# One core: attention scores in float32 for sixteen heads from operands of 128 rows, and a new fixed order of the whole program

## The chip, the cores and the metric

The program runs on one core of one Trainium2 chip. The time is what the device takes for one execution, in microseconds (us); lower is better. A core has five engines that run side by side, each through its own list of instructions in order: PE (TensorE, matrix multiplication; PEld is its loading of weights), DVE (VectorE), ACT (ScalarE), POOL (GpSimd) and SP (SyncE, which here only issues DMAs). PE's results go to PSUM; the other operands lie in SBUF, a memory of 128 partitions (rows).

## The reference

An attention with decay over 8 batches, 8 heads, 576 positions and 64 channels, and then a two-layer product with a cosine gate over the 4608 tokens.

```python
scores = scale * np.matmul(q, k.transpose(0, 1, 3, 2))
log_f = np.log(np.clip(f, 0.0001, 1.0))
cum = np.cumsum(log_f, axis=-1)
decay = cum[:, :, :, None] - cum[:, :, None, :]
scores = np.where(causal, -1000000000.0, scores + decay)
attn = softmax(scores)
x = (attn @ v) as (4608, 512)
h = x @ w_in                      # 512 -> 2048
out = (h * np.cos(h)) @ w_out     # 2048 -> 512
```

q, k, v and f are float32; both weights arrive as 64-bit floats.

## The kernel before

**The work.** Heads are taken in pairs, n = 0 to 31, four pairs to a batch. The first four pairs (n < N32 = 4) run `attention32`, all in float32; pairs 4 to 7 (n < NQ = 8) run `attention` with float32 scores; the other 24 run `attention` with scores from two products of rounded operands (L975 and L976). After each four pairs comes the two-layer product for that batch, in two halves of 320 and 256 tokens: `gemm1` (L1072, PE, three float16 products for each block) makes h, four steps on ACT and DVE (L1087 to L1093) make h times cos(h), L1100 and L1101 (or L1102) split it into two float16 parts g, and `gemm2` (L1118) multiplies these with the second weights.

**The float32 scores.** `load32` (L754 to L763) fills an operand tile for a head: 64 rows of q and k (L759, a DMA into partitions 0 to 63), 4 rows of decay (L760, a DMA into partitions 64 to 67, from a buffer `cum_d` in device memory), and 64 columns of zeros set by POOL (L758). The products are L818 (pairs 0 to 3) and L973 (pairs 4 to 7) and contract over 68 rows. The decay rows come out of a chain of their own at the start: load f (L586), clip, logarithm, running sum and split (L587 to L593), write to `cum_d` (L597).

**The weights.** The 32 tiles of the weights arrive as 64-bit words (L627, 512 KB each). DVE turns each into float32 in three steps (L617, L621, L625), ACT takes a bound of it (L636), and when a group's scale is known, ACT and DVE split it into two float16 parts (L646, L653). All 16 tiles of the second weights must be there before their scale is.

**v.** `prep_vscale` loads the four pairs of a batch once for a scale (L709, into a `stage` buffer), and `attention32` and `attention` load them again for the work (L769 or L906, buffer `v2`, two of them).

**The buffers.** Raw tiles of the second weights, the float32 operands of pairs 0 to 3 and g share a ring of 8 buffers named `g`; raw tiles of the first weights use `h`; the float32 operands of pairs 4 to 7 use `stage`.

**What sets the order.** Every operation is entered in a plan (`Plan.op`) with its engine, a cost and what it reads and writes. `order` runs a simulated schedule three times and then shifts due times by the table SHIFT; the last pass sets the place of each operation on its engine. Some operations have a second engine (`alt`): DVE or POOL for the subtractions, ACT or DVE for the copies out of PSUM (L777 and L778). Where PE is expected to wait in the first 200 us (FILL), the plan puts in pads: products of constant tiles (L1186) into a PSUM buffer that is about to be written, with no use for the result. The class `Clock` is the plan's picture of PE's clock, which in the profile is either 1.0 or 0.5 of full speed.

## Time and profile before

The time before is 1072.21 us, the median of 3 runs (1070.8 to 1072.59).

| | us |
|---|---|
| median of the runs | 1072.21 |
| the profiled execution, its own time | 1073.1 |
| its span, from the first to the last instruction | 1071.4 |
| PE busy | 1050.1 |
| ACT busy | 832.2 |
| DVE busy | 819.7 |
| POOL busy | 155.3 |
| pads, L1186 | 158 of them |

How to read the profile: a row names the line of the kernel, the engine, the operation, what it writes and reads, how often, the busy time in us and the mean of one in ns. The idle time is that of the engine just before these instructions, with what it waited for. A float32 product shows as two records, so 32 records are 16 products. Mean granted clock is given as PEclk. The tables by stretches give each engine's busy time with the number of records in brackets.

### The profile page before, as it was taken

How to read it: one execution, taken by the hardware profiler on the slowest of the kernel's cores; microseconds unless marked ns; L12 is line 12 of the kernel's file. 1: busy time of each engine (PE TensorE's matmuls, PEld its weight loads, DVE VectorE, ACT ScalarE, POOL GpSimd, SP SyncE). 2: the span in 40 equal slices, each digit the busy share in tenths (PEclk: the TensorE clock that was granted, in tenths of full speed). 3: DMA queues.
4: the chain of work that ended last, by engine and by line, in shares of the span. 5: the costliest groups of instructions: out<-in, count | busy, mean ns of one | idle time of the engine just before them, and what ended most of it. 6: DMA issues, size and time to landing. Idle time of an engine off the chain costs nothing. (4 is left out here: it accounts for less than half of the span.)

```text
span 1071.4 us, 23498 instructions
## 1 busy us (share of the span) xinstructions
PE 1050.1 (98%) x8975; PEld 841.6 (79%) x8975; DVE 819.7 (77%) x1801; ACT 832.2 (78%) x1739; POOL 155.3 (14%) x271
## 2 busy tenths in 40 slices
PE   8999999899999999999999999999999999999998
PEld 4778776688778887788778877778778877788787
DVE  6989999677887979678886879778776868671613
ACT  4758989588887989788888979887877978762522
...
PEclk9999999799999999999999999999999999999999
...
GB/s 267 309 284 109 99 135 102 126 162 158 180 152 147 139 142 167 149 101 159 182 154 144 127 148 167 169 129 130 178 144 144 134 142 75 85 59 21 7 20 20
DMA packets 256280, 146.37 MB, mean 137 GB/s; under 512 B 223337, under 2 KB 231529, under 8 KB 256169
## 3 DMA queue, kind: packets, MB, share of 16 engines
...
## 5 line engine op out<-in xcount | busy, mean ns | idle before, releaser
L1118 PE MATMUL hp<-g,W2s 128*128 128x256 f16 (+1 forms) x3072 | 390.9, 287 | 0.6 <-DVE W2s L653 0.4
L1072 PE MATMUL hp<-xh,W1s 128*128 128x256 f16 (+1 forms) x2048 | 380.4, 286 | 1.1 <-ACT h L1078 1.1
L1118 PEld LDWEIGHTS <-W2s 128*128 128x128 f16 x3072 | 297.9, 98 | 78.0 <-issue 0.8
L1072 PEld LDWEIGHTS <-W1s 128*128 128x128 f16 x3072 | 295.9, 98 | 78.6 <-issue 1.7
L1072 PE MATMUL hp<-xl,W1s 128*128 128x256 f16 (+1 forms) x1024 | 292.6, 286 | 0.0
L1013 DVE SCALAR_TENSOR_TENSOR PS<-pa,ri,PS 128x576 f16<-128x576 f32 (+2 forms) x280 | 140.7, 544 | 32.1 <-ACT PS L1009 31.3
L992 ACT ACTIVATE pa<-pa,nb 128x576 f32<-128x576 f32 (+2 forms) x280 | 141.1, 506 | 19.8 <-DVE nb L987 18.6
L987 DVE CUSTOM_DVE_ANT_0 pa<-pa,mask 128x576 f32<-128x576 f32 (+2 forms) x280 | 131.5, 513 | 31.8 <-PE pa L976 26.1
L1009 ACT ACTIVATE PS<-pa,ri 128x576 f16<-128x576 f32 (+2 forms) x280 | 134.1, 545 | 15.0 <-DMA pt<-PS 9.7
L1078 ACT ACTIVATE h<-hp 128x320 f32<-128x320 f32 (+1 forms) x256 | 101.3, 416 | 36.6 <-PE hp L1072 36.0
L1093 DVE TENSOR_TENSOR h<-h,r 128x1280 f32<-128x1280 f32 (+1 forms) x64 | 89.1, 1392 | 41.4 <-ACT r L1091 41.2
L997 POOL TENSOR_SCALAR ri<-L 128x1 f32<-128x1 f32 (+1 forms) x168 | 46.8, 279 | 410.4 <-ACT pa L992 404.9
L921 POOL TENSOR_TENSOR QK<-stage,QK 64x576 fp32r<-64x576 f32 x46 | 77.3, 1680 | 170.5 <-issue 116.4
L1091 ACT ACTIVATE r<-r,halfpi,m_inv 128x1280 f32<-128x1280 f32 (+1 forms) x64 | 86.2, 1347 | 18.8 <-DVE r L1089 18.3
L1101 DVE TENSOR_TENSOR g<-h,g 128x1280 f16<-128x1280 f32 (+1 forms) x62 | 84.2, 1358 | 14.1 <-ACT g L1100 13.7
L1087 DVE TENSOR_SCALAR r<-h,m_a 128x1280 int32<-128x1280 f32 (+1 forms) x64 | 56.8, 888 | 49.3 <-ACT h L1078 48.3
L1089 DVE SCALAR_TENSOR_TENSOR r<-r,m_b,h 128x1280 f32<-128x1280 int32 (+1 forms) x64 | 91.3, 1426 | 0.7
L975 PE MATMUL pa<-QK 128*128 128x288 f32 (+4 forms) x288 | 90.3, 330 | 1.5 <-DVE PS L1013 1.5
L1100 ACT CAST g<-h 128x1280 f16<-128x1280 f32 (+1 forms) x64 | 74.2, 1159 | 15.1 <-DVE h L1093 14.9
L1124 ACT ACTIVATE ot<-hp,m_o 128x320 f32<-128x320 f32 (+1 forms) x64 | 32.3, 504 | 65.9 <-PE hp L1118 50.4
L1042 PEld LDWEIGHTS <-vv 128*64 128x64 f16 x1512 | 69.4, 111 | 16.9 <-issue 14.2
L1042 PE MATMUL pa<-pt,vv 128*64 128x256 f16 (+2 forms) x1512 | 78.8, 256 | 3.7 <-DMA pt<-PS 3.4
(118 smaller groups left out, 1166.7 us busy)
## 6 DMA issues: line engine op xcount, KB each, us to landing
...
```

Of the source, the lines that this page charges most:

```text
L975: T.matmul(c, hi[:, 0, isl], hi[:, 1, d], start=True, stop=False)
L987: op("DVE", c_dve(w) + 0.008, lambda view=view, ib=ib, o=o, w=w, mk=mk, c=c: V.tensor_tensor_reduce(out=view(ib, o, w), in0=view(ib, o, w) ...
L992: op("ACT", c_act(w, True, 2), lambda view=view, ib=ib, o=o, w=w, c=c: A.activation(view(ib, o, w), view(ib, o, w), AF.Exp, bias=nb.get()[ ...
L1009: op("ACT", c_act(w, True, 1), lambda view=view, ib=ib, o=o, w=w, c=c, out_=out_: A.activation(out_(0), view(ib, o, w), AF.Copy, scale=ri. ...
L1013: op("DVE", c_dve(w) + 0.06, lambda view=view, ib=ib, o=o, w=w, c=c, out_=out_: V.scalar_tensor_tensor(out_(1), view(ib, o, w), ri.get()[: ...
L1042: T.matmul(d, vv.get()[:, jb, hd, kv], m, start=first and x == 0, stop=last and x == 2)
L1072: T.matmul(hp.get()[:, 0:w_], WS_[1][:, at(1, 4 * c + cb), w, fs], x.get(), start=(n == 0), stop=(n == 11))
L1078: op("ACT", c_act(w_, True), lambda hp=hp, k=k: A.activation(h.get()[:, k, 0:w_], hp.get()[:, 0:w_], AF.Copy, scale=float(2.0 ** -24)), re ...
L1089: op("DVE", c_dve(N) + 0.045, lambda: V.scalar_tensor_tensor(fl(r), fl(r).bitcast(I32), b1.get()[:, c:c + 1], fl(h), op0=ALU.mult, op1=ALU ...
L1091: op("ACT", c_act(N, aps=2), lambda: A.activation(fl(r), fl(r), AF.Sin, scale=inv.get()[:, c:c + 1], bias=halfpi), reads=[inv], writes=[r] ...
L1093: op("DVE", c_dve(N), lambda: V.tensor_tensor(fl(h), fl(h), fl(r), op=ALU.mult), reads=[r], writes=hk, prio=pr)
L1118: T.matmul(po.get()[:, 0:w_], WS_[2][:, at(2, 4 * c + k), w, msl], gh.get()[:, i, k, 0:w_], start=(n == 0), stop=(n == 47))
```

## The change

- **Operands of 128 rows.** The host packs q and k of batches 0 and 1 (pairs 0 to 7) into a new array `qk2` of 128 rows a head: rows 0 to 3 zero, rows 4 to 67 q and k, rows 68 to 127 zero. `load32` loads all 128 rows with one DMA (576 KB in place of 288 KB), and the decay rows are then written over rows 0 to 3. The products contract over 128 rows in place of 68, and the decay DMA now also waits for the load that it overwrites. POOL clears 128 rows in place of 68.
- **v of batch 0 once.** `load_v` loads each v tile once; `prep_vscale` of batch 0 takes its bound from the same `v2` tile (ACT, with a scratch tile in place of an overwrite). `v2` has 4 buffers in place of 2. Four DMAs of 320 KB go.
- **`g` has 7 buffers** in place of 8.
- **A turn table.** The table SHIFT and the passes `rank`, `backward` and `shift` go. TURN lists all operations in the order of their turn, and each engine takes the operation with the lowest turn among those that the simulated schedule has ready. SWAP lists the operations that run on their second engine. The plan's numbers change too: the clock's thresholds, how much a product counts as activity (`moving`), the DMA rate, and pads are allowed up to 240 us.

Counted in the two programs: pads 158 and 142 (91 and 77 of them before the first product of scores, then 67 and 49 before the first L1072, then none and 16 just ahead of the first L1118); copies L777 and L778 out of PSUM on DVE 15 and 9, on ACT 25 and 31; the subtraction for g on DVE 62 and 28, on POOL 2 and 36; the subtractions of q and k on DVE 37 and 33, on POOL 59 and 63; loads of activation tables on ACT 93 and 97. The lists after the last attention product are the same on PE.

```diff
-BUFS = dict(xs=1, stage=2, v2=2, vv=2, ..., g=8, ot=1,
+BUFS = dict(xs=1, stage=2, v2=4, vv=2, ..., g=7, ot=1,
-SHIFT = {
-    0: 2.6, 1: 50.9, 2: -45.6, 6: -4.6, 8: 39.7, 9: -8.9, 11: 124.1, 12: 13.5, 14: -37.1, 24: 47.5, 25: 4.9, 26: 33.8, 27: 46.2,
...
+TURN = (
+    20, 19, 62, 63, 84, 80, 81, 31, 352, 353, 82, 83, 69, 65, 66, 22, 21, 67, 68, 89, 85, 32, 86, 355, 354, 87, 37, 33, 88, 44, 169, 70,
...
+SWAP = {36, 43, 116, 115, 262, 346, 390, 473, 474, 569, 597, 649, 663, 1005, 1004, 1207, 1206, 701, 1290, 1289, 1054, 1333, 1332, 1372, 1373,
...
     def order(self):
-        self.rank()
...
-        self.shift()
-        return self.forward(0.0)[0]
+
+        for k, i in enumerate(TURN):
+            o = self.ops[i]
+            o.due = k
+            if i in SWAP:
+                o.eng, o.cost, o.fn = o.alt[:3]
+        return self.forward()
...
+    def load_v(n, pr):
+        if n not in V2:
+            b, p = divmod(n, NP)
+            v2 = V2[n] = ring("v2", [P, 5, P], F32)
+            op("SP", T_DGE, lambda: dma(v2.get(), vp[b, p].rearrange("p (j c) -> p j c", c=P)), writes=[v2], prio=pr, size=VSZ)
+        return V2[n]
...
+            if b == 0:
+                v2, jk = load_v(p, pr), ring("junk", [P, 640], BF16, tag="ot")
+                op("ACT", c_act(640, aps=1), lambda v2=v2, jk=jk, p=p: A.activation(
+                    jk.get(), v2.get().rearrange("p j c -> p (j c)"), AF.Square, accum_out=mx.get()[:, p:p + 1]),
+                   reads=[v2], writes=[mx.part(p), jk], prio=pr)
+                continue
...
-        op("POOL", 0.23, lambda: G.memset(q.get()[0:68, 0, 0:64], 0.0), writes=[q.part(0)], prio=pr - 1)
-        op("SP", T_DGE, lambda: dma(q.get()[0:64, :, ks], qkT[b, p, hd, 0:64]), writes=[q.part(1)], prio=pr - 1, size=DMQ)
-        op("SP", T_DGE, lambda: dma(q.get()[64:68, :, ks], cum_d[b * H + 2 * p + hd]),
-           reads=[CD.part((r, b > 0)) for r in range(4)], writes=[q.part(2)], prio=pr, size=DMC)
+        op("POOL", 0.23, lambda: G.memset(q.get()[:, 0, 0:64], 0.0), writes=[q.part(0)], prio=pr - 1)
+        op("SP", T_DGE, lambda: dma(q.get()[:, :, ks], qk2[b, p, hd]), writes=[q.part(1)], prio=pr - 1, size=DMQ)
+        op("SP", T_DGE, lambda: dma(q.get()[0:4, :, ks], cum_d[b * H + 2 * p + hd]),
+           reads=[CD.part((r, b > 0)) for r in range(4)], writes=[q.part(1), q.part(2)], prio=pr, size=DMC)
...
-                            T.matmul(c, qf.get()[0:68, 0, isl], qf.get()[0:68, 1, 64 + d.start:64 + d.stop], start=True, stop=True)
+                            T.matmul(c, qf.get()[:, 0, isl], qf.get()[:, 1, 64 + d.start:64 + d.stop], start=True, stop=True)
...
+    nb = NQ // NP
+    qk2 = np.zeros((nb, NP, 2, P, 2, S), qk.dtype)
+    qk2[:, :, :, 4:4 + D] = qk[:nb]
+    qkT = np.ascontiguousarray(np.concatenate([qk[nb:], qk[nb:]], axis=3))
```

Three places where the order of instructions moves. Below line 700 the lines of the changed kernel stand some 9 to 15 higher in number: L774 is the load of q and k (L759 before), L775 the decay rows (L760), L711 the load of v for the work, L724 the load of v for a scale (L709 before), L998 the masked sum of scores (L987 before), L1008 the scaling of a softmax's sums (L997), L1011 their reciprocals (L1000), L1024 the second part of the scaled probabilities (L1013), L1113 the subtraction for g on POOL (L1102).

The first place is SP's list of DMAs at the start. `vv` is the buffer for f, `cum_d<-pt` is a write of decay rows, and in_dram stands for any input. Before:

```order
L759 DMA g<-in_dram 64x2x576
L586 DMA vv<-in_dram 64x576
L627 DMA g<-in_dram 128x1024
L627 DMA h<-in_dram 128x1024
L709 DMA stage<-in_dram 128x640
L582 DMA cum_d<-pt_115 8x2x576
L582 DMA cum_d<-pt_123 8x2x576
```

And now:

```order
L586 DMA vv<-in_dram 64x576
L627 DMA h<-in_dram 128x1024
L711 DMA v_118<-in_dram 128x640
L582 DMA cum_d<-pt_112 8x2x576
L627 DMA g<-in_dram 128x1024
L724 DMA stage<-in_dram 128x640
L582 DMA cum_d<-pt_123 8x2x576
L774 DMA g<-in_dram 128x2x576
```

The load of f is first now, and the first q and k come seven places later. Between the second write of decay (L597) and the first read of it there stood a raw tile for `g`, one for `h` and a v tile; now there stand a v tile for a scale, a raw tile for `h`, a v tile for the work and a raw tile for `g`.

The second place is DVE's list where the last splits of the second weights (L653) stand, some 190 us into the program before. Before:

```order
L653 SCALAR_TENSOR_TENSOR W2s<-W2s,t_102 128x512
L1013 SCALAR_TENSOR_TENSOR PS_84<-pa_2110,ri,PS_84 128x448
L1013 SCALAR_TENSOR_TENSOR PS_85<-pa_2115,ri,PS_85 128x320
L1013 SCALAR_TENSOR_TENSOR PS_85<-pa_2110,ri,PS_85 128x64
L1013 SCALAR_TENSOR_TENSOR PS_85<-pa_2115,ri,PS_85 128x192
L1013 SCALAR_TENSOR_TENSOR PS_84<-pa_1936,ri,PS_84 128x576
L653 SCALAR_TENSOR_TENSOR W2s<-W2s,t_102 128x512
L714 TENSOR_REDUCE vmx<-stage 128x1 x2
L1093 TENSOR_TENSOR h<-h,r 128x4x256
L1050 SCALAR_TENSOR_TENSOR xl_2257<-pa_2067,xh_2248 128x256
L1087 TENSOR_SCALAR r<-h,m_a_1374 128x4x256
L653 SCALAR_TENSOR_TENSOR W2s<-W2s,t_102 128x512
```

And now, where six of the last splits stand close together:

```order
L653 SCALAR_TENSOR_TENSOR W2s<-W2s,t_102 128x512
L1011 RECIPROCAL ri<-ri 128x2
L653 SCALAR_TENSOR_TENSOR W2s<-W2s,t_102 128x512
L1024 SCALAR_TENSOR_TENSOR PS_84<-pa_1969,ri,PS_84 128x448
L653 SCALAR_TENSOR_TENSOR W2s<-W2s,t_102 128x512
L1024 SCALAR_TENSOR_TENSOR PS_85<-pa_1969,ri,PS_85 128x64
L653 SCALAR_TENSOR_TENSOR W2s<-W2s,t_102 128x512
L1024 SCALAR_TENSOR_TENSOR PS_85<-pa_1972,ri,PS_85 128x320
L653 SCALAR_TENSOR_TENSOR W2s<-W2s,t_102 128x512
L1024 SCALAR_TENSOR_TENSOR PS_85<-pa_1972,ri,PS_85 128x192
L653 SCALAR_TENSOR_TENSOR W2s<-W2s,t_102 128x512
L1100 SCALAR_TENSOR_TENSOR r<-r,m_b_1368,h 128x4x256
```

Ahead of the last split DVE has fewer instructions now: six copies L778, five L1013, three L714 (a bound of v), and one each of L1087, L1093, L1101, L1050 and L933 stand behind it or on another engine, and the masked sums of two blocks too.

The third place is POOL's list from its first subtraction for g on. Before, at the same place:

```order
L997 TENSOR_SCALAR ri<-L 128x1
L758 MEMSET stage 68x64
L997 TENSOR_SCALAR ri<-L 128x2 x2
L997 TENSOR_SCALAR ri<-L 128x1 x2
L997 TENSOR_SCALAR ri<-L 128x2 x4
L758 MEMSET stage 68x64 x2
```

And now:

```order
L1008 TENSOR_SCALAR ri<-L 128x1
L773 MEMSET stage 128x64
L1008 TENSOR_SCALAR ri<-L 128x2 x2
L1008 TENSOR_SCALAR ri<-L 128x1
L1113 TENSOR_TENSOR g<-h,g 128x1280
L1008 TENSOR_SCALAR ri<-L 128x1
L1008 TENSOR_SCALAR ri<-L 128x2 x3
L1113 TENSOR_TENSOR g<-h,g 128x4x256
```

Subtractions for g now stand between the scalings of softmax sums, which run in order behind them.

127 lines of the change are left out of this document (29 added, 98 removed), and 307 rows, old and new, of tables (SHIFT, SWAP, TURN).

## The prediction

> **What bounds the kernel now.** First the page: busy shares and the clock granted to PE.
>
> ```profile
> span 1071.4 us, 23498 instructions
> PE 1050.1 (98%) x8975; PEld 841.6 (79%) x8975; DVE 819.7 (77%) x1801; ACT 832.2 (78%) x1739; POOL 155.3 (14%) x271
> PEclk9999999799999999999999999999999999999999
> ```
>
> PE is busy 98% of the span, so time can only be gained where PE does nothing, does pads, or runs at half its clock. The table by stretches shows where (length, busy us of PE, PEld, DVE, ACT and POOL, clock, DMA share, GB/s):
>
> ```profile
> 0.00:21.02 21.02, 18.73 (x92) 9.42 (x92) 12.47 (x23) 7.39 (x17) 4.87 (x24) 1.00 0.81 263
> 21.02:56.57 35.55, 31.83 (x198) 23.47 (x197) 32.71 (x98) 27.51 (x81) 0.85 (x6) 1.00 0.93 298
> 56.57:59.98 3.41, 3.41 (x11) 2.19 (x11) 2.69 (x11) 1.74 (x5) 0.00 (x0) 0.50 1.02 206
> 59.98:114.29 54.31, 52.34 (x367) 44.04 (x366) 52.77 (x162) 40.51 (x120) 2.46 (x13) 1.00 0.57 173
> 140.00:189.69 49.69, 44.34 (x363) 32.83 (x362) 48.56 (x110) 46.13 (x94) 3.76 (x13) 1.00 0.52 119
> 189.69:203.34 13.65, 12.62 (x54) 8.04 (x54) 9.82 (x21) 6.34 (x13) 0.19 (x1) 0.50 0.57 138
> 203.34:300.00 96.66, 96.66 (x881) 79.17 (x880) 75.50 (x167) 82.21 (x172) 22.03 (x31) 1.00 0.70 152
> 300.00:1040.00 740.00, 736.30 (x6569) 598.91 (x6568) 548.57 (x1141) 586.18 (x1175) 119.65 (x181) 1.00 0.58 127
> 1040.00:1071.38 31.38, 28.13 (x258) 24.96 (x256) 11.25 (x10) 10.14 (x17) 0.00 (x0) 0.98 0.05 18
> ```
>
> Length less PE's busy time gives the idle time: 2.29, 3.72, 0, 1.97, 5.35 and 1.03 us up to 203.34, together 14.4; after that only 3.70, and 3.25 at the end. Two stretches, 3.41 and 13.65 us, run at half the clock: (3.41 + 13.65) / 2 = 8.5 us lost. From 21 to 190 us DVE is busy 32.71 of 35.55, 52.77 of 54.31 and 48.56 of 49.69 us, so there PE waits for what DVE hands it. The rest are pads:
>
> ```profile
> L1186 PE MATMUL pa<-mask,ones 128*128 128x448 bf16 x123 | 25.6, 367 | 2.9 <-POOL ones L497 2.3 <-ACT PS L836 0.6
> L1186 PE MATMUL hp<-mask,ones 128*128 128x448 bf16 x35 | 8.9, 371 | 0.9 <-DVE pt L778 0.9
> 48.85 4.51 PE L1186 MATMUL pa<-mask,ones 128*128 128x448 bf16 x23
> 54.43 3.80 PE L818 MATMUL pa<-g 68*128 68x288 f32 x12 [1.06 <-DMA g<-in_dram]
> ```
>
> Pads fill 25.6 + 8.9 = 34.5 us; 23 in a row took 4.51, so one takes 0.196. Up to 203 us PE thus loses 14.4 + 8.5 + 34.5 = 57.4 us, and only 7 after it. The change is weighed by what it does to these 57.
>
> **The change part by part**, as changes of lost time, each with its bounds.
>
> **1. The start.** The first score product waits for the decay rows, behind 91 pads.
>
> ```profile
> 0.80 0.70 SPq L759 DMA_DIRECT2D g<-in_dram  x1
> 1.55 0.58 SPq L586 DMA_DIRECT2D vv<-in_dram  x1
> 13.41 0.38 SPq L709 DMA_DIRECT2D stage<-in_dram  x1
> L818 PEldq EVENT_SEMAPHORE  x4: 51/51/51, 19.8 to 54.3; - x4
> ```
>
> PE's queue has its data at 19.8, but the pads hold the product until 21.02: 1.2 us are free to win. With 77 pads PE could start 14 x 0.196 = 2.7 earlier. For the rest the decay rows must come sooner: f's load goes first, 1.55 - 0.80 = 0.75 us earlier, while one DMA more stands between the write and the read of the decay (about 0.4 to issue, as at 13.41, and 320 KB more ahead). I take **-2.0**, between -1.2 and -2.7. DVE's first masked sum moves with it.
>
> **2. Pads after that** up to the first L1072: 67 become 49, 18 x 0.196 = 3.5 us. A pad left out is a wait that the plan no longer expects; where the wait stays, PE idles instead and nothing is won. **-1.7**, between 0 and -3.5.
>
> **3. Loads and the half clock at 57 us.** A load of 64 rows is slow and slows what runs beside it:
>
> ```profile
> 40.00:44.00 4.00, 3.40 (x25) 2.38 (x24) 4.00 (x9) 3.92 (x15) 0.00 (x0) 1.00 1.01 394
> 54.00:60.00 6.00, 5.57 (x20) 3.79 (x21) 4.24 (x15) 3.13 (x8) 0.00 (x0) 0.72 1.06 212
> ...
> 53.71 1.23 SPq L759 DMA_DIRECT2D stage<-in_dram  x2
> ```
>
> From 40 to 44 us, with weights and v alone in flight, full queues move 394 GB/s; from 54 to 60, with loads L759 among them, 212. At these rates 288 KB take 1.4 us and 576 KB would take 1.5, so the doubled bytes cost about nothing and the weights beside them run faster; the four v loads dropped save 1.28 MB / 394 GB/s = 3.2 us of queue. Of the 3.72 us idle from 21 to 57 I take **-1.0** (0 to -1.6, the wait of 1.06 above and one more like it).
> The clock: tables by stretches of 3.41 us, the length of the first slow stretch and a quarter of the second.
>
> ```profile
> 53.16:56.57 3.41, 2.35 (x11) 1.59 (x10) 2.37 (x5) 1.81 (x6) 0.15 (x1) 1.00 1.03 219
> 77.05:80.46 3.41, 3.41 (x19) 2.55 (x18) 3.17 (x10) 0.98 (x2) 0.12 (x1) 1.00 0.97 346
> 193.10:196.52 3.42, 3.42 (x9) 2.22 (x8) 1.69 (x3) 0.94 (x1) 0.00 (x0) 0.50 0.91 174
> 199.93:203.34 3.41, 3.41 (x14) 1.93 (x13) 2.58 (x5) 1.60 (x7) 0.19 (x1) 0.50 0.44 172
> 192.62 5.88 PE L973 MATMUL pa<-stage 68*128 68x448 f32 x12 [1.03 <-DMA stage<-in_dram]
> ```
>
> After a window with 2.35 us busy, nearly all in 68-row products, the clock halves at 56.57; after a full one at 77.05 it holds. From 193.10 to 196.52 PE is busy all the time with 68-row products (L973) and the clock stays at half; the window from 199.93, full of float16 products of 128 rows, brings it back. So 68 rows seem to count for less, and 128 rows should hold or bring back the clock sooner. **-1.7** here (0 to -1.7).
> The Trainium skill, "TensorE: Matmul & The Clock Gate", Part 1 (The HAM clock gate), ties the clock to how busy PE was in a free-running window of 3413 ns and names no rows. The stretches agree with its window; that window from 193.10, busy and still slow, does not fit busyness alone. By that rule rows would change nothing: the first rival.
>
> **4. 140 to 190 us, 5.35 us idle.** What DVE still has to do ahead of the last split L653 shrinks:
>
> ```profile
> L778 DVE COPY pt<-hp 128x512 f32<-128x512 f32 (+2 forms) x15 | 7.9, 536 | 1.1 <-ACT pt L777 0.8 <-PE hp L789 0.3
> L714 DVE TENSOR_REDUCE vmx<-stage 128x1 f32<-128x640 f32 x4 | 3.2, 812 | 0.0
> L1013 DVE SCALAR_TENSOR_TENSOR PS<-pa,ri,PS 128x576 f16<-128x576 f32 (+2 forms) x280 | 140.7, 544 | 32.1 <-ACT PS L1009 31.3
> L1093 DVE TENSOR_TENSOR h<-h,r 128x1280 f32<-128x1280 f32 (+1 forms) x64 | 89.1, 1392 | 41.4 <-ACT r L1091 41.2
> L1101 DVE TENSOR_TENSOR g<-h,g 128x1280 f16<-128x1280 f32 (+1 forms) x62 | 84.2, 1358 | 14.1 <-ACT g L1100 13.7
> ```
>
> Six copies L778 are 3.2 us, five L1013 2.7, three L714 2.4, one each of L1093 and L1101 2.8: 11.1 us, before the small ones. Ahead of the first four W2 splits the sums about cancel (the six copies go, one round of L1087 to L1093 comes), so the first L1118 comes no sooner than the start gives, and the plan puts 16 pads (3.1 us) before it. Behind it, waits for late splits and softmaxes should go. -5.35 + 3.1 = **-2.2**, between -5.35 and +3.1.
>
> **5. The half clock at 190 us.** It begins while PE stands idle for a late transposed softmax:
>
> ```profile
> 189.66 1.92 PE L1042 MATMUL pa<-pt,vv 128*64 128x64 f16 x23 [2.30 <-DMA pt<-PS]
> ```
>
> With those earlier, or with 128-row products that bring the clock back, 13.65 / 2 = 6.8 us and some of the 1.03 idle go: **-7.0**, between 0 and -7.8.
>
> **6. What the change costs.** 34 subtractions for g move to POOL, and ACT loads 97 tables in place of 93.
>
> ```profile
> L1102 POOL TENSOR_TENSOR g<-h,g 128x1024 f16<-128x1024 f32 x2 | 4.3, 2135 | 18.7 <-ACT g L1100 18.7
> L1091 ACT ACT_TABLE_LOAD x4 | 5.1, 1283 | 0.1
> L976 PEld LDWEIGHTS pa<-QC 68*128 68x128 f32 x288 | 54.8, 190 | 0.8
> L975 PEld LDWEIGHTS pa<-QK 128*128 128x128 f32 x288 | 54.7, 190 | 7.6 <-issue 2.0 <-POOL ri L997 0.7
> ```
>
> A g part comes 2.14 - 1.36 = 0.8 us later or more, on a POOL busy 14%; DVE gains 34 x 1.36 = 46 us. Four table loads are 5.1 us on an ACT busy 78%; they cost up to that where PE waits for ACT. PE's work ahead covers both, as it covers the present waits (3.7 us idle from 300 to 1040); without that cover the 0.8 us would come up to 34 times. Rows cost PE nothing: weights of 68 and of 128 rows load in 190 ns. The decay DMA's new wait holds up the DMAs behind it on SP, but it stands well behind its load in the list. A `g` buffer less can hold up a raw tile; DMA is at 0.57 share from 60 us on. **+1.5**, between 0 and +5.
>
> **The sum.** -2.0 - 1.7 - 1.0 - 1.7 - 2.2 - 7.0 + 1.5 = -14.1. Against the profiled execution's own time (1073.1, of which 1071.4 is span) that is 1059.0; the median, 1072.2, lies 0.9 lower, so **1058**. All best ends give -22.4, or 1050.
>
> **The rivals.**
> - **The clock stays as it is:** only busyness counts, or a new gap opens at the same place. Terms 5 and the clock part of 3 fall: -14.1 + 7.0 + 1.7 = -5.4, 1067. For it: the window from 53.16 was also only 2.35 us busy. Against it: 193.10 to 196.52.
> - **Slower, by POOL's order.** A subtraction for g now stands ahead of a softmax's scaling (L997), and L1000, L1009, L1013, the transposes and L1042 follow it. Where that chain has less than 2.1 us in hand, PE idles after 203 us, where it now idles 3.7 us in 740. Each hit costs up to 2.1; seven of the 36 eat the whole gain, ten give 1058 + 21 = 1079. For it: the row of L975 above already has 0.7 us that POOL's L997 ended last; against it: PE has 96.66 + 736.30 = 833 us of work there and waits 3.7. The Trainium skill, "SBUF — State Buffer", section "SBUF: two separate sides", says that DVE and GpSimd lock a shared port pair for a whole instruction and the loser waits. By it DVE could lose up to 36 x 2.1 = 76 us to these where it gains 46; at 77% busy DVE would still not be the bound, so it makes this rival a little likelier and no more.
> - **Nothing comes of it:** missing pads turn into idle time, DVE stays as late. 1071.
>
> **How the numbers follow.** Forecast 0.62, its own range 1050 to 1064; clock unchanged 0.20; slower 0.12; nothing 0.06. A measurement tells about 0.2% (2.1 us) from no change. Faster 0.82, same 0.06, slower 0.12. The range runs from 1050 to 1072, leaving out the slower case and a few in a hundred below.
>
> **What would show it.** Right: the first score product near 19 us; no half clock near 57 us and near 190; fewer than 8 us idle up to 205 us; 4 us idle or less from 300 to 1040 us. A load of 128 rows at 350 GB/s or more beside weights supports term 3. Wrong: half-clock stretches as long as now while PE is busy with 128-row products; L1042 or L1118 waiting on POOL's chain late in the program; idle time where pads were.

## The result and the profile after

The changed kernel is slower. Its time is **1080.84 us** (median of 4 runs, 1079.71 to 1082.39) against 1071.76 for the kernel before (4 runs): a ratio of 1.0086, 95% interval 1.0069 to 1.0103. The forecast of 1058 was wrong in its sign, and the time lies above its range. The profiled execution took 1080.46 us, 7.4 more than that of before (1073.1).

First the page of the changed kernel: the span, the busy shares and the granted clock.

```profile
span 1078.7 us, 23423 instructions
PE 1044.6 (97%) x8959; PEld 838.5 (78%) x8959; DVE 784.6 (73%) x1757; ACT 844.6 (78%) x1749; POOL 241.1 (22%) x309
PEclk9899999999999999999999999999999999999999
```

Some of the announced effects are there: DVE is busy 35 us less, POOL 86 more, and the half clock near 57 and near 190 us is gone. A new one stands from 25.71 to 35.95 us (length, busy us of PE, PEld, DVE, ACT and POOL, clock, DMA share, GB/s):

```profile
25.71:35.95 10.24, 6.65 (x24) 4.98 (x24) 8.54 (x22) 5.78 (x20) 0.49 (x3) 0.50 1.01 383
```

The table by stretches, in the same columns and with the borders used for the kernel before:

```profile
0.00:21.02 21.02, 17.74 (x83) 9.03 (x84) 14.88 (x23) 10.32 (x24) 4.88 (x24) 1.00 0.88 323
21.02:56.57 35.55, 27.60 (x164) 21.65 (x163) 31.95 (x91) 24.85 (x74) 0.80 (x5) 0.86 0.95 347
59.98:114.29 54.31, 49.86 (x345) 41.12 (x346) 51.55 (x168) 45.60 (x132) 2.23 (x10) 1.00 0.45 155
140.00:189.69 49.69, 45.98 (x363) 33.50 (x362) 46.62 (x108) 47.00 (x95) 7.28 (x13) 1.00 0.53 112
189.69:203.34 13.65, 12.06 (x87) 8.56 (x86) 8.70 (x16) 11.15 (x20) 5.79 (x6) 1.00 0.67 173
203.34:300.00 96.66, 95.21 (x857) 77.63 (x856) 72.17 (x164) 80.38 (x164) 30.37 (x33) 1.00 0.70 164
300.00:1040.00 740.00, 732.79 (x6543) 595.08 (x6541) 520.15 (x1118) 592.05 (x1184) 188.16 (x212) 1.00 0.56 126
```

Length less PE's busy time: 3.28, 7.95, 4.45, 3.71 and 1.59 us idle in the first five rows, where before had 2.29, 3.72, 1.97, 5.35 and 1.03. Then 1.45 and 7.21, where it had 0 and 3.70. So PE idles more almost everywhere; only 140 to 190 us gained, by 1.6. Up to 203 us it idles 22.2 us where before had 14.4, and from there to 1040 us 8.7 where it had 3.7: 12.8 us more in all. The pads, by line and buffer:

```profile
L1195 PE MATMUL pa<-mask,ones 128*128 128x448 bf16 x82 | 18.2, 388 | 2.3 <-POOL ones L497 2.3
L1195 PE MATMUL hp<-mask,ones 128*128 128x448 bf16 x60 | 12.5, 352 | 0.0
```

That is 30.7 us of pads, 3.8 less than the 34.5 before.

Busy time hides where a program falls behind, because pads and products at half clock count as busy. So one more measure was worked out from each trace: the time at which PE has done a given share of its useful work (every product but the pads, each counted by its columns, float32 records twice). The difference between two kernels at the same share is the **lag**. For the changed kernel against before, in us:

```
time in before    60.8  119.4  160.0  181.8  210.1  284.0  355.6  610.8  721.2  1061.3
lag of after      -1.9   +4.8   +7.4   +8.8   +1.7   +3.1   +4.6   +8.5   +6.9    +7.3
```

Each lag is that of one execution. By these points the kernel loses 6.7 us between 61 and 119 us and 4.0 more to 182, wins 7.1 where before ran at half clock, and loses 5.6 after 210 us. The first point is a lucky one, since before stands in 23 pads and a half clock just ahead of it (from 48.85 us on). Worked out in the same way, the lag is about -1.5 us at 22, +6.8 at 30, +7.8 at 42, -0.2 at 62, +5.0 at 66, -0.2 at 78 and +2.4 at 94 us. So there is a loss ahead of 61 us too, which is made up again and comes back. Split by what PE did, the +7.3 us at the end are +12.8 of idle time, -3.0 of pads, -5.2 for products at half clock, and 2.7 that stay unexplained.

The first of these losses, PE's timeline at the start (start, length, operation, in brackets the idle time before it and what ended it):

```profile
19.44 3.08 PE L831 MATMUL pa<-g 128*128 128x288 f32 x12 [0.97 <-DMA g<-cum_d]
27.42 0.27 PE L569 MATMUL hp<-dg,ones 128*128 128x128 bf16 x1 [4.90 <-DVE dg L566]
27.48 2.77 PE L802 MATMUL hp<-eyef,PS 128*128 128x128 f32 x12
32.13 0.90 PE L802 MATMUL hp<-eyef,PS 128*128 128x128 f32 x3 [1.88 <-ACT pt L790]
34.69 4.52 PE L831 MATMUL pa<-g 128*128 128x288 f32 x16
...
174.47 3.19 PE L1195 MATMUL hp<-mask,ones 128*128 128x448 bf16 x16
177.50 5.05 PE L1129 MATMUL hp<-g,W2s 128*128 128x320 f16 x36
```

and the counterparts of the second head and of L1129 in the kernel before:

```profile
26.66 3.08 PE L818 MATMUL pa<-g 68*128 68x288 f32 x12 [0.56 <-DMA g<-in_dram]
166.75 3.42 PE L1118 MATMUL hp<-g,W2s 128*128 128x320 f16 x24
```

The first product comes at 19.44 instead of 21.02. But the second head's products (L831, L818 before) come at 34.69, where the kernel before had them at 26.66, and 4.90 + 1.88 us of idle time lie in between. At 174.47 the 16 new pads stand, 3.19 us, and the first L1129 starts at 177.50; its counterpart L1118 started at 166.75. SP's queue tells what is new (what waited, for what: us in all, times, longest), from 10 to 60 us:

```profile
SPq L775 <- DMA g<-in_dram: 6.0, 4, 3.2
```

The read of the decay rows waits for the load that it overwrites. Before, L760 has no such row; the two are independent there. From 61 to 120 us PE waits 4.7 us in all, 3.9 of them for the exponentials of the softmax (L849, ACT), and these in turn wait for DVE's masked sums (nb, L839; waits of ACT, 61 to 120 us):

```profile
ACT PS L849 <- DVE nb L839: 4.7, 4, 2.1
```

### The profile page after: what moved, and what is told of

It is laid out like the page before. It is cut to its first block, busy times and chain, and to the rows that moved or that the text cites. A ratio compares the mean times of both kernels' runs of the same rounds, so it can differ in the third digit from the quotient of the medians.

```text
span 1078.7 us, 23423 instructions
## 1 busy us (share of the span) xinstructions
PE 1044.6 (97%) x8959; PEld 838.5 (78%) x8959; DVE 784.6 (73%) x1757; ACT 844.6 (78%) x1749; POOL 241.1 (22%) x309
## 4 chain that ended last, share of the span: by engine, by line
PE 52%; ACT 6%; DMA 3%; DVE 3%; issue 1%; POOL 0%; SPq 0%; ACTq 0%; POOLq 0%
PE hp L1129 24%; PE hp L1083 18%; PE pa L1053 4%; DMA pt<-PS 3%; PE pa L986 3%; PE pa L987 2%; ACT PS L1020 1%; ACT pa L1003 1%; ACT r L1102 1%; ACT L1102 1%; ACT h L1089 1%; ACT L1003 1%; DVE PS L1024 1%; DVE pa L998 1%; DVE r L1098 0%
## 5 line engine op out<-in xcount | busy, mean ns | idle before, releaser
L1129 PE MATMUL hp<-g,W2s 128*128 128x256 f16 (+1 forms) x3072 | 388.4, 286 | 1.2 <-ACT ot L1135 0.8
L1129 PEld LDWEIGHTS <-W2s 128*128 128x128 f16 x3072 | 296.7, 98 | 77.4 <-issue 1.7
L1024 DVE SCALAR_TENSOR_TENSOR PS<-pa,ri,PS 128x576 f16<-128x576 f32 (+2 forms) x280 | 141.6, 543 | 52.1 <-ACT PS L1020 51.8
L1003 ACT ACTIVATE pa<-pa,nb 128x576 f32<-128x576 f32 (+3 forms) x280 | 141.0, 504 | 35.2 <-DVE nb L998 34.1
L998 DVE CUSTOM_DVE_ANT_0 pa<-pa,mask 128x576 f32<-128x576 f32 (+3 forms) x280 | 132.2, 510 | 36.3 <-PE pa L987 28.5
L1089 ACT ACTIVATE h<-hp 128x320 f32<-128x320 f32 (+1 forms) x256 | 101.4, 414 | 30.9 <-PE hp L1083 30.1
L1113 POOL TENSOR_TENSOR g<-h,g 128x1280 f16<-128x1280 f32 (+1 forms) x36 | 91.0, 2529 | 150.1 <-ACT g L1111 150.0
L1008 POOL TENSOR_SCALAR ri<-L 128x1 f32<-128x1 f32 (+1 forms) x168 | 43.2, 257 | 346.4 <-ACT pa L1003 331.2
L1098 DVE TENSOR_SCALAR r<-h,m_a 128x1280 int32<-128x1280 f32 (+1 forms) x64 | 61.9, 967 | 54.1 <-ACT h L1089 53.2
L1100 DVE SCALAR_TENSOR_TENSOR r<-r,m_b,h 128x1280 f32<-128x1280 int32 (+1 forms) x64 | 97.1, 1518 | 0.9
L1102 ACT ACTIVATE r<-r,halfpi,m_inv 128x1280 f32<-128x1280 f32 (+1 forms) x64 | 86.3, 1348 | 13.8 <-DVE r L1100 13.2
L1111 ACT CAST g<-h 128x1280 f16<-128x1280 f32 (+1 forms) x64 | 73.8, 1154 | 14.1 <-DVE h L1104 13.3
L987 PE MATMUL pa<-QC 68*128 68x288 f32 (+4 forms) x288 | 76.5, 304 | 0.0
```

The source lines that it names most:

```text
L987: T.matmul(c, co[0:68, 0, isl], co[0:68, 1, d], start=False, stop=True)
L998: op("DVE", c_dve(w) + 0.008, lambda view=view, ib=ib, o=o, w=w, mk=mk, c=c: V.tensor_tensor_reduce(out=view(ib, o, w), in0=view(ib, o, w) ...
L1003: op("ACT", c_act(w, True, 2), lambda view=view, ib=ib, o=o, w=w, c=c: A.activation(view(ib, o, w), view(ib, o, w), AF.Exp, bias=nb.get()[ ...
L1024: op("DVE", c_dve(w) + 0.06, lambda view=view, ib=ib, o=o, w=w, c=c, out_=out_: V.scalar_tensor_tensor(out_(1), view(ib, o, w), ri.get()[: ...
L1089: op("ACT", c_act(w_, True), lambda hp=hp, k=k: A.activation(h.get()[:, k, 0:w_], hp.get()[:, 0:w_], AF.Copy, scale=float(2.0 ** -24)), re ...
L1100: op("DVE", c_dve(N) + 0.045, lambda: V.scalar_tensor_tensor(fl(r), fl(r).bitcast(I32), b1.get()[:, c:c + 1], fl(h), op0=ALU.mult, op1=ALU ...
```

## The experiments

Two theories stood at first. A: POOL's order (the rival of the prediction), subtractions for g ahead of softmax scalings. B: the start, where the decay read's new wait and the new order put PE's work late. Later runs asked what the rows, the pads and the order each are worth. All kernels compute all of the reference; "order" means the lists of all engines with the choice of engine and the pads, frozen as printed tables. Kernels made from the changed one have its line numbers, those made from before have before's. Ratios are to the kernel before, timed beside each on the same chip; its medians were 1070.4 to 1073.4, so two kernels of different batches are better compared by their ratios than by their medians. The changed kernel's ratio is 1.0086 (1.0069 to 1.0103).

| run | what | median, us | ratio, 95% interval |
|---|---|---|---|
| e3 | after, g subtractions on DVE | 1080.92 | 1.0064 (1.0040 to 1.0088) |
| e2 | after, 64 rows loaded, 68-row products | 1087.40 | 1.0104 (1.0056 to 1.0153) |
| e6 | after, 112 rows loaded, 116-row products | 1088.38 | 1.0152 (1.0136 to 1.0168) |
| e4 | after, 124 rows loaded | 1146.98 | 1.0671 (1.0633 to 1.0710) |
| e1 | before, 124 rows loaded, 128-row products | 1143.72 | 1.0635 (1.0596 to 1.0675) |
| e5 | before, 112 rows loaded, 116-row products | 1074.34 | 1.0005 (0.9988 to 1.0022) |
| e10 | before, 128 rows loaded, decay wait | 1089.71 | 1.0179 (1.0162 to 1.0195) |
| e11 | e10 and 12 pads at 190 us | 1092.98 | 1.0207 (1.0191 to 1.0222) |
| h0 | after's parts in before's order | 1105.25 | 1.0293 (1.0265 to 1.0321) |
| h1 | new order to 205 us, then old | 1083.21 | 1.0091 (1.0068 to 1.0114) |
| h2 | old order to 205 us, then new | 1118.17 | 1.0418 (1.0390 to 1.0446) |
| h3 | new order to 328 us, then old | 1081.42 | 1.0090 (1.0073 to 1.0107) |
| h4 | before to 325 us, then new order | 1080.76 | 1.0084 (1.0063 to 1.0104) |
| e13 | after without 47 pads | 1082.73 | 1.0109 (1.0091 to 1.0127) |
| e9 | before and 12 pads at 187 us | 1071.15 | 0.9998 (0.9978 to 1.0017) |
| e14 | before and 20 pads at three places | 1070.69 | 0.9976 (0.9953 to 0.9999) |
| e12 | after, two out buffers | 1078.07 | 1.0063 (1.0047 to 1.0080) |
| e15 | e12, g subtractions on DVE | 1079.51 | 1.0055 (1.0036 to 1.0074) |

Nine of the eighteen came out slower than every range that had been expected of them: e1, e4, e6, e10, e11, h0, h1, h2 and h4.

**1. POOL's subtractions.** e3 puts all 36 back on DVE, at the same places in the program.

```diff
-alt=("POOL", 0.9 * c_pool(N), lambda: G.tensor_tensor(gx(1), fl(h), gx(0), op=ALU.subtract), SLG))
+alt=("POOL", 0.9 * c_pool(N), lambda: V.tensor_tensor(gx(1), fl(h), gx(0), op=ALU.subtract), SLG))
```

> The changed kernel with the 36 subtractions for g that run on POOL done by DVE, at the same places of the fixed order; all other lists unchanged. If POOL's slow subtractions (2.5 us each, ahead of the softmax scaling, and slowing DVE beside them) are what costs the 5 us of new idle time after 203 us, this is about 1075 to 1077 us. If the order alone is at fault, the idle time stays: 1079 to 1083, or more, since DVE gets some 50 us of work.

1080.92 us, the median of the changed kernel. By the ratios e3 would be 0.22% ahead of it, some 2 us, with intervals that overlap; e15 against e12, the same exchange, is 0.08% ahead by ratio and 1.4 us behind by median. So by these figures the subtractions cost some 2 us or nothing, and theory A falls as the cause of the 9. They do slow DVE: of L1098 and L1100, in the groups of the changed kernel,

```profile
L1100 DVE SCALAR_TENSOR_TENSOR r<-r,m_b,h 128x1280 f32<-128x1280 int32 (+1 forms) x64 | 97.1, 1518 | 0.9
L1098 DVE TENSOR_SCALAR r<-h,m_a 128x1280 int32<-128x1280 f32 (+1 forms) x64 | 61.9, 967 | 54.1 <-ACT h L1089 53.2
```

and of e3,

```profile
L1100 DVE SCALAR_TENSOR_TENSOR r<-r,m_b,h 128x1280 f32<-128x1280 int32 (+1 forms) x64 | 92.8, 1450 | 0.8
L1098 DVE TENSOR_SCALAR r<-h,m_a 128x1280 int32<-128x1280 f32 (+1 forms) x64 | 56.4, 882 | 46.6 <-ACT h L1089 45.7
```

L1100 takes 68 ns more in the changed kernel and L1098 85. That is 64 x 0.153 = 9.8 us of DVE, of which the kernel's time shows some 2 us or nothing.

**2. The rows.** e2 goes back to 64 loaded rows and products over 68, without the decay read's wait, in the new order.

```diff
-op("SP", T_DGE, lambda: dma(q.get()[:, :, ks], qk2[b, p, hd]), ...
+op("SP", T_DGE, lambda: dma(q.get()[4:68, :, ks], qk2[b, p, hd, 4:68]), ...
-T.matmul(c, qf.get()[:, 0, isl], qf.get()[:, 1, 64 + d.start:64 + d.stop], start=True, stop=True)
+T.matmul(c, qf.get()[0:68, 0, isl], qf.get()[0:68, 1, 64 + d.start:64 + d.stop], start=True, stop=True)
```

> The changed kernel with its own order on every engine, and only the operands as before: 64 rows loaded, 68 rows multiplied, so the decay read has no load to wait for. If the order is what lost (idle time after 203 us and pads and idle before), the time is as slow as the changed kernel, about 1081, or slower by up to 7 us where half-clock stretches come with 68 rows (1081 to 1088). If the wide loads and the decay read's wait for them lost it, the second head's products come near 27 us and not at 34.7, and the time falls to 1071 to 1076.

1087.4 us, 6.6 above the changed kernel by the median; but its runs go from 1078.15 to 1091.01, and its ratio's interval takes in that of the changed kernel, so a gain from the 128 rows is not shown in the time. Nor does the second head come sooner without the wait: it starts at 36.21 us, after 7.38 us of idle time ahead of L569. What e2 shows is the clock. Two windows of 3.41 us with nearly the same products and the same busy time of PE in them (in e2, 1.45 of the 1.73 us are products of 68 rows), and the windows that follow; the changed kernel, by stretches:

```profile
100.80:104.21 3.41, 1.74 (x10) 1.08 (x9) 3.29 (x18) 3.00 (x11) 0.00 (x0) 1.00 0.01 5
104.21:107.63 3.42, 3.42 (x24) 2.99 (x24) 3.38 (x14) 3.29 (x11) 0.78 (x5) 1.00 0.07 7
```

and e2:

```profile
64.37:67.78 3.41, 3.41 (x9) 2.34 (x9) 2.71 (x8) 0.95 (x3) 0.00 (x0) 0.50 0.97 362
67.78:71.19 3.41, 3.41 (x10) 2.39 (x9) 0.73 (x2) 1.05 (x6) 0.00 (x0) 0.50 0.93 309
112.15:115.56 3.41, 1.73 (x10) 1.21 (x8) 3.29 (x17) 3.41 (x14) 0.00 (x0) 1.00 0.00 0
115.56:118.98 3.42, 3.42 (x16) 3.14 (x15) 2.46 (x9) 2.37 (x8) 0.55 (x3) 0.50 0.23 48
57.54:60.95 3.41, 3.41 (x18) 3.41 (x17) 1.83 (x4) 1.26 (x4) 0.29 (x2) 0.50 0.16 61
```

With 1.74 us busy over 128 rows the clock holds; with 1.73 us over 68 rows for the most part it halves. And two windows in a row, nearly full of 68-row products, stay at half. In e10 (below) the same products over 128 rows fill a window at half clock,

```profile
68.28:71.69 3.41, 3.41 (x9) 2.20 (x8) 1.80 (x5) 0.83 (x2) 0.00 (x0) 0.50 0.92 297
```

and the half clock ends with it, at 71.69 us. Rows are not all: the last row of e2 above is full of L876, products of 128 rows but of 64 columns, and the clock stays at half. The Trainium skill, "TensorE: Matmul & The Clock Gate", Part 1 (The HAM clock gate), ties the clock to how busy PE was in such a window; the length of the windows agrees with it, but these rows do not fit busyness alone.

e1, e4, e5 and e6 load other numbers of rows, all from row 4 on, so that the decay read waits for nothing: rows 4 to 127 (124 rows), or 4 to 115 (112 rows).

```diff
-op("SP", T_DGE, lambda: dma(q.get()[:, :, ks], qk2[b, p, hd]), ...
+op("SP", T_DGE, lambda: dma(q.get()[4:P, :, ks], qk2[b, p, hd, 4:P]), ...
```

That is e4. e1 makes the same operands in before's order, with the decay rows over 0 to 3 and products over all 128; e5 and e6 have 4:116 for 4:P, and 0:116 in the products.

> The kernel before with its own order of instructions on every engine, and only the float32 operands changed: rows 4 to 127 are loaded (zeros from row 68 on), the decay rows lie in rows 0 to 3, and the products contract over 128 rows. If rows count for the clock (term 3 and 5 of the prediction), the two half-clock stretches of the kernel before, 3.4 us at 57 us and 13.7 us at 190 us, go, and the time is about 1063 to 1065 us. If only busyness counts, both stay and the time is 1070 to 1073. If the doubled bytes of the loads are what made the changed kernel slow, this one is slow too: up to 16 loads by the 0.7 us that 288 KB more take at 390 GB/s, 11 us, 1075 to 1083.

> The changed kernel, where the loads of the float32 operands take rows 4 to 127 only, so the read of the decay rows into rows 0 to 3 no longer waits for them; bytes, rows and order stay. If that wait is what starves PE from 22 to 35 us (the read of the second head's decay stands at 28.25 us behind a load issued at 19.39), the second head's products come 2 to 6 us sooner, the half clock at 26 us ends sooner and the time is 1075 to 1079. If the load itself lands that late, nothing changes: 1080 to 1082.

> The kernel before with its own lists on every engine; the float32 operands alone are changed: 112 rows are loaded into rows 4 to 115 (7 rows for each of 16 engines, where 124 rows went to few of them), decay in rows 0 to 3, products over 116 rows. No read of decay waits for a load. If more rows hold the clock, both half-clock stretches go: 1063 to 1067, with a granted clock of 0.998 or more in every run. If the half clock at 190 us costs little because PE waits there anyway (runs of the kernel before at a clock of 0.995 and 0.992 differ by about 1 us only), 1069 to 1072 at a higher clock. If wide loads cost more than they give, 1074 or more.

> The changed kernel in its own order, but rows 4 to 115 are loaded and 116 rows multiplied, so the read of the decay rows has no load to wait for. If that new wait starves PE at the start (second head's decay read at 28.25 us, products at 34.69), the products come 1 to 4 us sooner and the time is 1076 to 1080. If the load that the products need is itself that late, the time is 1080 to 1082 as for the changed kernel.

The 124-row loads were meant to take the wait away and change little else, and the kernels took 1144 and 1147 us instead. PE waits for the decay rows that stand behind such loads (waits of PE up to 200 us, e4):

```profile
PE pa L831 <- DMA g<-cum_d: 34.3, 4, 11.7
```

and where these loads are nearly alone in flight, e4 by stretches shows

```profile
45.00:53.00 8.00, 3.30 (x10) 1.73 (x11) 4.34 (x9) 1.36 (x4) 0.21 (x1) 0.50 0.26 103
```

a DMA share of 0.26 and 103 GB/s: a quarter of the engines, kept busy. The Trainium skill, "DMA: Bandwidth & Descriptors", section "Why a DMA increments its semaphore by 16 and not by 1", says that a DMA uses the largest number of engines, up to 16, that divides its slowest dimension; for 124 rows that is 4 of 16, and the share agrees. The expectation had overlooked this. With 112 rows all engines work (e5 has a DMA share of 0.95 from 5 to 60 us), but a packet of 2304 bytes takes 145 ns on the mean in e5 and 134 in e6, against 99 in the changed kernel (packet records, first 80 us). So e6 cannot settle what the wait costs, since its loads are slower; its second head starts at 35.89 us, no sooner than in the changed kernel. e5 has no wait, slower loads, and 116 rows: 1074.34, no different from before. In its profile the half clock at 57 us is gone and that near 190 shorter, from 193.81 to 204.05 us, but PE idles more. On balance, more rows in the old order bring nothing.

**3. Parts and order apart.** h0 runs all parts of the change (128 rows with the wait, v once, 7 buffers `g`) in the order of before with its 158 pads; h1 to h4 change the order at one point. e10 and e11 have 128 rows and the wait alone, in before's order, where 8 of 16 decay reads had to move 1 to 5 places back to stand behind their loads. Only the tables differ:

```diff
-TURN = (
-    0, 6, 54, 16, 29, 1, 3, 74, 349, 7, 4, 8, 30, 59, 55, 56, ...
+PADS = {32: 91, 97: 7, 100: 3, 122: 4, 153: 3, 212: 23, 215: 2, 222: 4, 234: 2, 237: 4, 248: 1, 268: 6, 365: 5, 376: 1, 525: 2}
+for i in TURN:
+    o = self.ops[i]
+    o.fn, o.pads = o.alt[2] if i in SWAP else o.fn, PADS.get(i, 0)
+    out.append(o)
```

> The changed kernel's parts (128-row operands with the decay read's wait, v of batch 0 loaded once, 7 buffers for g) in the order of the kernel before, with its choice of engines and its 158 pads; a few DMAs and operations on the first 120 us move where the new buffers demand it. If the order alone makes the changed kernel slow, this is at most the time of before: 1062 to 1072. If the parts make it slow, 1077 to 1083.

> The changed kernel's own order up to about 205 us, then the order and the engines of the kernel before (2 of the later subtractions for g on POOL in place of 34). If the new order loses its 5 to 6 us between 210 and 600 us, this is 1074 to 1076, and the rest of the loss lies ahead of the cut. If what follows 205 us is late because the state at the cut is bad (less work ready ahead of PE), the waits come back in the old order too: 1079 to 1082.

> The reverse: the order of the kernel before up to about 205 us, on the changed kernel's parts, then the new order with its engines. If the new order loses 5 to 6 us after 210 us by itself, this is 5 to 6 us above the kernel with the parts in the old order; if the start is what matters, it is within 1.5 us of it.

> The changed kernel's own order for the first quarter of PE's work (to about 328 us), then the order and engines of the kernel before. The cut lies behind all float32 scores, where both orders have the same work in hand. If the new order itself loses time after 205 us (its lag behind the kernel before grows from 1.7 us at 212 us to 8.5 us at 600 us), the lag stays at the 4 us it has at the cut: 1075 to 1078. If the parts or a bad start cause it, the lag grows on: 1079 to 1082.

> The kernel before, unchanged in parts and order for the first quarter of PE's work (to about 325 us), then the new order and its engines (27 subtractions for g on POOL), with 18 loads of v moved on SP because v2 has two buffers. If the new order is what loses, the lag grows by about 4 to 5 us between 325 and 600 us: 1075 to 1078, from a start that nothing touched. If the loss needs the new start or the new parts: 1071 to 1073.

> The kernel before in its own order on PE, DVE, ACT and POOL, with full 128-row loads of the float32 operands and 128-row products; the decay rows are written over rows 0 to 3, and 8 of the 16 reads of decay stand 1 to 5 places behind their load on SP where they stood ahead of it. If 128 rows are free in the loads (93 ns for a packet of 2304 bytes in place of 158), PE is at the place of the kernel before at 60 and 120 us within 1 us, and the time is 1069 to 1073. If the bytes and the wait of the decay reads cost, the start is 3 to 6 us later and the time 1074 to 1078.

> The same, with the 12 pads ahead of the waiting L1042 near 190 us as well. If rows hold the clock where 68-row windows dropped it and the pads hold it at 190 us, nearly all runs show a clock of 0.998 or more and the time is 5 to 6 us under the kernel with the full loads alone. If the clock drops at other places by the phase of its windows, the gain is 1 to 2 us, as with the pads alone (0.9998).

The lag of each behind before, from their traces, in us:

```
time in before   60.8  119.4  181.8  210.1  284.0  355.6  610.8  721.2  1061.3
after            -1.9   +4.8   +8.8   +1.7   +3.1   +4.6   +8.5   +6.9    +7.3
e5               +1.5   +4.2   +4.2   +2.8   +3.1   +3.2   +3.2   +3.5    +3.6
h0               +8.0  +33.2  +33.2  +31.9  +32.5  +32.3  +32.4  +30.9   +32.1
e10             +13.0  +14.8  +14.8  +17.6  +18.2  +18.5  +18.5  +16.7   +16.9
h1               -2.3   +3.5   +7.2   +6.8   +9.0   +9.3  +10.3   +9.3    +9.9
h3               -2.6   +3.7   +7.3   +1.6   +2.9   +9.3  +10.4   +9.2    +9.6
h4               +1.4   +1.5   +1.5   +1.4   +1.3   +1.9   +7.3  +11.5   +10.6
h2              +11.4  +30.4  +30.4  +35.2  +38.0  +38.5  +43.3  +45.3   +45.0
```

First, **the wait is dear in before's order**. In e10 SP stands still for it (its queue, 10 to 60 us),

```profile
SPq L760 <- DMA g<-in_dram: 11.5, 2, 7.5
```

and PE waits for what stands behind (PE, up to 200 us):

```profile
PE pa L818 <- DMA g<-cum_d: 8.0, 3, 4.6
```

e10 is 13.0 us late at 61 us, where e5, without the wait and with slower packets, is 1.5 late. So the wait, with the reads that were moved for it, costs some 11.5 us there. In h0 most reads stand right behind their load, and it loses 33; its SP, from 10 to 130 us:

```profile
SPq L775 <- DMA g<-in_dram: 40.1, 7, 7.9
```

The new order gives back most of that: 33.2 becomes 4.8 at 119 us. So it can be read as a repair, in good part, for the change's own wait.

Second, **the two ends of the order are separate**. h0 loses nothing after 119 us: in the old order the changed parts cost nothing there. h3 loses time at its cut, from 328 us (half clock from 326 to 333), and is flat from 356 on; its time, 1081.42, lies where it was expected for a bad start, but with 6.4 us of it lost at the cut it can't tell the two apart. h4, which is before until 325 us, loses 8.7 us after it, and h2 loses 10 after 210. Of h4's loss 3.2 us are a half clock from 706.56 to 713.38 us (PE busy 6.31 us in it) that the changed kernel doesn't have, and its profiled execution, 1083.64 us, was slower than its median. The idle time of PE from 355 to 1040 us is a steadier measure. In the old order it is 3.3 us (before), 2.9 (h0), 3.1 (h3) and 3.8 (h1), and 2.0 to 4.9 over all ten kernels, of which e9 has the most. In the new one it is 5.6 (after), 8.4 (h4) and 8.1 (h2), and 4.8 to 8.4 over all eight with one out buffer (see 4), of which e3 has the least. So the new order itself idles more after 330 us, whatever came first; the two ranges touch, so one execution alone would not show it. By stretches, before, after and then h4:

```profile
355.00:1040.00 685.00, 681.68 (x6076) 554.55 (x6075) 505.51 (x1043) 540.03 (x1079) 108.90 (x163) 1.00 0.57 125
```

```profile
355.00:1040.00 685.00, 679.37 (x6063) 552.06 (x6061) 483.30 (x1037) 548.09 (x1089) 169.84 (x191) 1.00 0.56 124
```

```profile
355.00:1040.00 685.00, 676.61 (x5997) 548.74 (x5996) 480.62 (x1026) 543.82 (x1085) 168.15 (x190) 1.00 0.56 125
```

**4. The out buffer.** The waits of PE from 203 to 1040 us are 13 in the waits of the changed kernel, the longest of 2.1 us, and go back to several chains: h (L1089), the scaled probabilities (L1024), the reciprocal (L1011), the split x (L1061). One of them is the copy of the result out of PSUM on ACT, which waits for its only buffer `ot` to be stored (waits of ACT, 203 to 1040 us):

```profile
ACT ot L1135 <- DMA out_dram<-ot: 13.8, 14, 1.9
```

Before has 13.4 us there, but in 6 waits. e12 gives `ot` a second buffer and pays with one of 8 for each of xh1 and xl1; e15 is e12 with the subtractions on DVE.

```diff
-BUFS = dict(..., xh1=8, xl1=8, h=3, r=1, g=7, ot=1,
+BUFS = dict(..., xh1=7, xl1=7, h=3, r=1, g=7, ot=2,
```

> The changed kernel with two output buffers (ot) in place of one, and 7 of the buffers xh1 and xl1 in place of 8 to make room; every list is unchanged. ACT's waits for the store of the output before (6.5 us from 300 to 700 us) go. If they are what delays ACT's chain in the new order, the 5 us of idle time on PE after 203 us fall to about 2 and the time is 1076 to 1079. If the order's waits on DVE and PE remain, 1079.5 to 1082.

> The changed kernel with two output buffers and the 36 subtractions for g on DVE, every other list unchanged. If POOL's long subtractions still hold up the softmax scaling, this is 1 to 3 us below the kernel with two output buffers (about 1078): 1075 to 1077. If they are hidden, it is within 1 us of it.

1078.07 us, 2.8 less than the changed kernel, and 1079.51, 1.4 less than e3; by the ratios 0.23% and 0.09%, or 2.5 and 1.0 us. The idle time from 355 to 1040 us falls to that of the old order, 3.0 (e12) and 2.65 (e15):

```profile
355.00:1040.00 685.00, 682.02 (x6079) 554.94 (x6077) 481.31 (x1028) 546.05 (x1091) 170.07 (x190) 1.00 0.56 124
```

So the single buffer may account for some 1 to 3 of the 5.6 us lost late. The ratios of e12 and of the changed kernel overlap at their edges (1.0047 to 1.0080 and 1.0069 to 1.0103), e3 has the ratio of e12 without a second buffer, the profiled execution of e12 (1074.53 us) was the fastest of its six, and a second buffer in before's order was not tried. So this points to the buffer and doesn't prove it.

**5. The pads.** e13 takes out all pads of the changed kernel from 60 us on, the 16 at 174 us among them. e9 adds 12 to the kernel before, ahead of L1042 at 187 us, where the half clock began. e14 adds 3 at 26 us and 5 at 53 us to these.

```diff
-PADS = {32: 77, 97: 5, 119: 2, 122: 11, 215: 17, 234: 7, 365: 5, 477: 2, 664: 16}
+PADS = {32: 77, 97: 5, 119: 2, 122: 11}
```

```diff
-            for _ in range(o.pads):
+            for _ in range(o.pads + MORE.get(o.id, 0)):
```

with `MORE = {921: 12}` in e9 and `{98: 3, 214: 5, 921: 12}` in e14.

> The changed kernel without its pads from 60 us on (17, 7, 5, 2, and 16 ahead of the first L1118: 47 pads, 9.2 us). If pads there hold PE back, the time falls by some of the 9 us: 1072 to 1078. If they only fill waits, PE idles in their place and the time stays at 1080 to 1082, or rises to 1083 to 1090 where the clock drops in the empty windows.

> The kernel before with 12 more pads (2.35 us) on PE just ahead of the transposed-softmax products L1042 that wait 2.30 us at 189.66, so that PE is busy in the window in which the clock is lost. Nothing else changes. If the half clock from 189.7 to 203.3 costs what term 5 says (13.65 us at half the clock, 6.8 us), the stretch stays at full clock and the time is 1064 to 1067. If PE waits for other engines in that stretch anyway, the clock is held and the time is 1070 to 1072.

> The kernel before with 20 more pads in three waits for DMA that its trace shows ahead of PE's work: 3 at 26.1 us (0.56 us idle), 5 at 53.4 us (1.06 us) and 12 ahead of the L1042 near 190 us (2.30 us). If these are the places where the clock drops, most runs show 0.998 or more and the median is 1066 to 1069, below both kernels. If it drops elsewhere, by the phase of its windows, it stays at 1070 to 1072.

e13 has 47 pads less, about 9 us of them, and gains nothing: 1082.73. So what these pads leave is filled by waits. e9's profile shows what pads can do. PE's timeline:

```profile
187.04 2.43 PE L1186 MATMUL pa<-mask,ones 128*128 128x448 bf16 x12
190.25 1.08 PE L1042 MATMUL pa<-pt,vv 128*64 128x64 f16 x23 [0.63 <-DMA pt<-PS]
```

and by stretches:

```profile
186.28:189.69 3.41, 3.34 (x20) 1.72 (x19) 3.41 (x5) 2.87 (x4) 0.29 (x2) 1.00 0.92 120
189.69:203.34 13.65, 12.07 (x113) 9.09 (x112) 11.40 (x27) 10.65 (x23) 3.49 (x5) 1.00 0.64 158
```

The window before 189.69 is full, the next 13.65 us run at full clock, and the trace is 5.5 us ahead at 210. But that is one execution: over 12 runs the median is 1071.15, no gain, since the clock still falls in most of them. The runs of e14 show it: 1065.85 and 1067.06 at a mean clock of 1.000, 1076.54 to 1077.98 at 0.990 to 0.994. Its median, 1070.69, lies 0.24% under the kernel before beside it (0.01% to 0.47%). It is the only kernel ahead of both, and barely. On e10 the same 12 pads bring nothing either (e11, 1092.98 against 1089.71).

## Why the prediction was wrong

The terms as predicted, and the change of the lag in the stretch of each:

| step | expected | measured |
|---|---|---|
| 1, the start (first product 21.02, then 19.44) | -2.0 | -1.6 |
| 2 and 3, pads, loads and clock, to 119 us | -4.4 | +6.4 |
| 4, 119 to 182 us | -2.2 | +4.0 |
| 5, the half clock at 190 us | -7.0 | -7.1 |
| 6, costs, after 210 us | +1.5 | +5.6 |
| sum | -14.1 | +7.3 |

**Terms 1 and 5 came out by their numbers.** The first product comes "near 19 us", and there is no half clock near 57 and 190. But the gain of term 1 doesn't last: behind the first products PE stands idle for 4.90 us, and the lag is +6.8 us at 30. For 5 the reason was only half right. 128 rows alone don't take that half clock away. In before's order it comes back in e10 at the same place in the work and as long as ever,

```profile
204.81:218.47 13.66, 7.19 (x31) 4.81 (x26) 5.53 (x11) 3.67 (x4) 0.00 (x0) 0.50 0.50 125
```

since PE does nothing in almost half of it. 116 rows leave 10.24 us of it standing (e5), and 12 pads alone take it away in a profile (e9): it starts from a window in which PE is mostly idle, and in the changed kernel the emptiest window near 190 us is still 1.82 of 3.41 us busy (from 199.79). That -7.1 came out against -7.0 is in part luck, since of the two reasons given, earlier work and more rows, the second alone doesn't do it; and e3, in the new order as well, has 3.41 us of half clock from 202.66. Rows do count for the clock (e2, e10), as step 3 argued from the row at 193.10, so the rival "the clock stays as it is" falls for these two places. But the half clock from 25.71 to 35.95 us, which costs some 3 us (half of PE's 6.65 us in it), was in no term.

**The loads of term 3 were right, its gain wasn't.** That "the doubled bytes cost about nothing" holds for the rate; the DMA of after from 5 to 60 us, and of before:

```profile
DMA packets 6839, 19.24 MB, mean 350 GB/s; under 512 B 712, under 2 KB 712, under 8 KB 6835
```

```profile
DMA packets 5668, 16.20 MB, mean 295 GB/s; under 512 B 670, under 2 KB 670, under 8 KB 5664
```

3 MB more arrive in the same time. But the waits that PE has at the start are 0.97 us for decay rows, then 4.90 and 1.88 us for DVE and ACT, and none of them is for the bytes of a load.

**The sign was lost where PE's waits were expected to shrink.** Steps 2 to 4 counted on it, and step 6 put the costs at 1.5. PE's idle time grew by 12.8 us instead, and the pads and the half clock give back some 8 of it. Two steps of the prediction failed.

The first is the sentence of step 6 that the decay DMA's new wait "stands well behind its load in the list", priced at nothing. In the changed kernel six DMAs do stand between the two, but a load issued at 19.39 has landed only when L775 goes out at 28.25, with the queues full, and everything behind waits with it on SP. In before's order this wait costs some 11.5 us by 61 us (e10 against e5). The new order lives with it by putting the second head 8 us later; PE's list then reaches L569 and L802 before DVE and ACT have done their part, and the clock halves from 25.71 to 35.95 us. How much of the +6.4 is the wait, in the new order, stays open: the runs that took it away there (e2, e4, e6) also changed the loads. That e2 and e6 have the same hole ahead of L569 (7.38 and 4.35 us) and a second head at 36.21 and 35.89 us speaks for the order rather than the wait as the cause of that hole.

The second is steps 2 and 4, where pads left out were counted as gain and 11.1 us taken off DVE as an end to PE's waits. PE's idle time from 21 to 114 us rose from 5.7 us to 12.7, and pads taken out bring nothing (e13). At 174 us the plan needs 16 pads and still starts the first L1129 10.75 us later. The trace shows DVE with 20 weight conversions (L625) begun by 60 us, where it had 17, and the softmax steps behind them: PE's waits from 61 to 120 us go back to DVE's masked sums. That the earlier conversions are the reason was not tested.

**Term 6 was too small.** Of its parts the subtractions on POOL cost some 2 us or nothing (e3, e15), where the second rival needed 14 to 21. The 5.6 us lie with the new order (h4 loses 8.7 on an untouched start, 3.2 of them in a half clock), and the single `ot` buffer may hold some 1 to 3 of them (e12, e15). The rest is spread over waits of up to 2.1 us on several chains, and no single cause was found.

The tests that the prediction named decide as they were meant to: 22 us idle up to 203 us (asked: fewer than 8), 7.2 us from 300 to 1040 (asked: 4 or less), and "idle time where pads were". The rival "slower, by POOL's order" ended near the measured time, by a cause that e3 rules out. "Nothing comes of it" had one thing right, that missing pads turn into idle time, and no loss.
